# A new order for the opening of a windowed-attention and max-out FFN kernel, up to its first regular slot

## The chip, the cores and the metric

The kernel runs on one core of one Trainium2 chip. The metric is the device time of one execution in microseconds (us). The kernel before takes 179.86 us (median of three runs, 179.77 to 180.04).

A core has engines that work side by side and hand over by semaphores. PE (TensorE) multiplies matrices and transposes; its weight loads are shown apart as PEld. DVE (VectorE), ACT (ScalarE) and POOL (GpSimd) do elementwise work. SP (SyncE) issues most DMA transfers, and POOL some. Each engine executes its instructions strictly in the order in which the program issued them, so an instruction that waits also holds all that stand behind it on that engine. The results of PE go to PSUM, which has eight banks.

## The reference

Inputs are q, k, v of shape (4 batches, 8 heads, 768 positions, 64), four weight matrices in float32, a sink count of 4 and a window of 128.

```python
scores = (1 / np.sqrt(D)) * np.matmul(q, k.transpose(0, 1, 3, 2))
rel = pos[:, None] - pos[None, :]
keep = (pos[None, :] < n_sink) | ((rel >= 0) & (rel < window))
a = softmax(np.where(keep, scores, -1e9))
x = np.matmul(a, v)                      # then heads are merged: (3072, 512)
h = np.maximum(np.maximum(x @ w1, x @ w2), x @ w3)     # (3072, 768)
out = h @ w_out                                        # (3072, 512)
```

## The kernel before, in words

**Tiling.** The 3072 rows are worked on in 12 chunks of 256 positions, three for each batch. A chunk's attention looks at its own keys, at the second half of the chunk before it, and at the four sink positions of its batch (the first chunk of a batch needs neither). The eight heads are handled as four pairs, 0 to 3. "Group" 0 of K or Q holds pairs 0 and 1, group 1 holds pairs 2 and 3.

**Steps of a chunk.** Each is a small function, and `n` or `ci` is the chunk:

- `load` (L76) issues one transfer of 512 KB on SP for each of K, Q and V. There are two raw buffers for each of the three. A `gate` first writes one element of the buffer on POOL, so that the transfer waits for POOL to come to that place; `pool_gate` (L441) writes a zero there, `after(wi)` (L435) copies an element of weight matrix `wi`, and so waits for that weight to land as well.
- `cast_qk` (L95, row L101) and `cast_v` (L104, row L105) convert to bf16; K and Q have two parts for each chunk, V four.
- `turn` and `turn2` (L109, L129) transpose K or Q on PE (rows L115, L137) and copy the result from PSUM on the engine named (rows L119, L122, L141, L144). `turn_dma` (L150) does the same by transposing DMA transfers on SP: two for K (L159) and one for Q (L154). Chunks 0 to 3 are turned on PE, chunks from 4 on by DMA.
- `premask` (L252, row L257) writes an additive mask into PSUM before the scores. `score` (L260, row L275) computes the scores of a pair, `expo` (L283, row L287) the exponentials on ACT, `mask` (L290, row L293) multiplies by a 0/1 mask on DVE where there was no additive one.
- `sink_k` (POOL, L226), `sink_v` (L311), `sink_score` (L295) and `av_open` (L325) handle the four sink positions.
- `av` (L340) multiplies with V on PE (row L351) and normalises on DVE (L356, L359). `xpose` (L365, on PE, row L372) or `xpose_dma` (L376, on SP, row L378) transposes the result x for the FFN.
- `ffn_h(ci, fp, wi)` (L384) is one block of the hidden layer: 8 matmuls (row L391) for a third of the hidden columns and one of three weights. For `wi` 0 ACT copies the block out (L398), for 1 and 2 DVE takes the maximum (L402).
- `ffn_y` (L407) is the output of half a chunk: six matmuls (row L412) and a copy (L414) by DVE or, with no engine named, by ACT. `store` (L427, row L428) writes a chunk's output, 512 KB, from SP.

**Weights.** `load_w` (L236, row L239) and `load_wo` (L244) load pieces of the four weight matrices by transfers from POOL's queue, converted to bf16 on the way.

**What sets the order.** The whole program is scheduled by hand: the order of the calls is the order on every engine and every queue. L455 to L656 write out the opening, which is everything up to the transposes of chunk 3's x, one call after another. Then a loop runs over slots: slot i (from 3) holds the FFN's output of chunk i-1, its hidden layer for chunk i and the attention of chunk i+1. The branch for i = 3 (L665), the first regular slot, is written out apart; the later slots have three other branches. `RING` = 4 sets of turned K, turned Q and converted V are kept. `sinks(n)` calls `sink_k` and `sink_v` in the slot of a batch's second chunk, and `cast(n)` puts all eight casts of a chunk on POOL.

Of the kernel before, what the change touches and what calls it, by code (L numbers as in the profile page):

```python
# [16 lines left out]
def kernel(  # L17
# [13 lines left out]
    nc = tc.nc  # L31
# [11 lines left out]
    NCH = B * CPB  # L43
# [5 lines left out]
    with tc.manual_schedule():  # L49
# [404 lines left out]

        masks()  # L455
        load(0, 'k')
        cast_qk(0, 'k', 1, nc.scalar)
        warm(9)
        premask(0, (2,))
        cast_qk(0, 'k', 0, nc.vector)  # L460
        load(0, 'q')
        load(0, 'v', gate=pool_gate)
        turn(0, 'k', 0, nc.scalar)
        turn(0, 'k', 1, nc.scalar)
        sink_init()
        cast_qk(0, 'q', 1, nc.vector)
        cast_qk(0, 'q', 0, nc.vector)
        premask(0, (3,))
        turn(0, 'q', 1, nc.vector)
        premask(0, (1,))  # L470
        turn(0, 'q', 0, nc.vector)
        cast_v(0, 0, 0, nc.vector)
        masks_late()
        cast_v(0, 1, 1, nc.gpsimd)
        score(0, (2,))
        cast_v(0, 1, 0, nc.vector)
        score(0, (1,))
        load_w(0, 512, 768)
        expo(0, 2)
        load(1, 'k')  # L480
        cast_v(0, 0, 1, nc.vector)
        load_w(0, 0, 512)
        load(1, 'q')
        score(0, (3,))
        cast_qk(1, 'k', 0, nc.vector)
        expo(0, 3)
        expo(0, 1)
        premask(0, (0,))
        av_open(0)
        score(0, (0,))  # L490
        av(0, 2)
        cast_qk(1, 'k', 1, nc.gpsimd)
        av(0, 3)
        expo(0, 0)
        turn2(1, 'k', 0, nc.scalar)
        av(0, 1)
        cast_qk(1, 'q', 1, nc.gpsimd)
        load_w(1, 512, 768)
        cast_qk(1, 'q', 0, nc.vector)
        turn2(1, 'k', 1, nc.scalar)  # L500
        load_w(1, 0, 512)
        av(0, 0)
        premask(1, (1,))
        turn2(1, 'q', 0, nc.vector)
        load(1, 'v')
        turn2(1, 'q', 1, nc.vector)
        xpose(0, 0, nc.vector)
        score(1, (0,))
        score(1, (1,))
        cast_v(1, 1, 0, nc.vector)  # L510
        score(1, (2,))
        expo(1, 0)
        cast_v(1, 1, 1, nc.vector)
        xpose(0, 1, nc.vector)
        cast_v(1, 0, 1, nc.vector)
        sink_k(0)
        expo(1, 2)
        premask(1, (3,))
        sink_v(0)
        sink_score(1)  # L520
        cast_v(1, 0, 0, nc.gpsimd)
        load_w(2, 512, 768)
        mask(1, 0)
        score(1, (3,))
        expo(1, 1)
        ffn_h(0, 2, 0)
        av_open(1)
        expo(1, 3)
        mask(1, 2)
        load(2, 'k', gate=after(0, 300))  # L530
        load(2, 'q', gate=pool_gate)
        load_w(2, 0, 256)
        av(1, 0)
        av(1, 1)
        av(1, 2)
        ffn_h(0, 0, 0)
        av(1, 3)
        ffn_h(0, 1, 0)
        xpose(1, 1, nc.vector)
        xpose(1, 0, nc.vector)  # L540
        ffn_h(0, 2, 1)
        ffn_h(1, 1, 0)
        load(2, 'v', gate=after(1))
        cast_qk(2, 'k', 1, nc.vector)
        ffn_h(1, 2, 0)
        load_w(2, 256, 512)
        ffn_h(1, 0, 0)
        ffn_h(1, 2, 1)
        load(3, 'q', gate=after(0))
        ffn_h(1, 0, 1)  # L550
        cast_qk(2, 'q', 1, nc.scalar)
        load_wo(0, 3)
        load_wo(3, 6)
        cast_qk(2, 'q', 0, nc.scalar)
        ffn_h(0, 0, 1)
        ffn_h(0, 1, 1)
        cast_qk(2, 'k', 0, nc.scalar)
        ffn_h(0, 2, 2)
        turn(2, 'k', 1, nc.vector)
        load(3, 'k', gate=after(1))  # L560
        ffn_h(1, 0, 2)
        ffn_h(1, 2, 2)
        ffn_h(1, 1, 1)
        ffn_h(0, 0, 2)
        turn(2, 'q', 0, nc.scalar)
        turn(2, 'q', 1, nc.vector)
        turn(2, 'k', 0, nc.vector)
        ffn_h(1, 1, 2)
        ffn_h(0, 1, 2)
        load(3, 'v', gate=after(2))  # L570
        sink_score(2)
        cast_v(2, 0, 1, nc.gpsimd)
        score(2, (3,))
        score(2, (1,))
        score(2, (2,))
        score(2, (0,))
        expo(2, 3)
        expo(2, 0)
        expo(2, 1)
        load(4, 'k', gate=after(2))  # L580
        mask(2, 3)
        cast_v(2, 1, 0, nc.vector)
        cast_qk(3, 'q', 1, nc.gpsimd)
        cast_v(2, 1, 1, nc.gpsimd)
        ffn_y(0, 0, nc.vector)
        expo(2, 2)
        mask(2, 0)
        cast_qk(3, 'q', 0, nc.scalar)
        ffn_y(0, 1)
        cast_v(2, 0, 0, nc.vector)  # L590
        mask(2, 2)
        mask(2, 1)
        cast_qk(3, 'k', 0, nc.scalar)
        ffn_y(1, 0)
        turn(3, 'q', 1, nc.scalar)
        turn(3, 'q', 0, nc.vector)
        av_open(2)
        cast_qk(3, 'k', 1, nc.gpsimd)
        cast_v(3, 1, 0, nc.gpsimd)
        av(2, 2)  # L600
        cast_qk(4, 'k', 0, nc.gpsimd)
        av(2, 0)
        av(2, 3)
        av(2, 1)
        ffn_y(1, 1)
        load(4, 'v')
        turn(3, 'k', 0, nc.vector)
        turn(3, 'k', 1, nc.scalar)
        load(4, 'q')
        xpose(2, 0, nc.vector)  # L610
        xpose(2, 1, nc.vector)
        score(3, (1,))
        expo(3, 1)
        score(3, (3,))
        cast_qk(4, 'k', 1, nc.vector)
        cast_v(3, 0, 1, nc.vector)
        expo(3, 3)
        score(3, (0,))
        score(3, (2,))
        mask(3, 1)  # L620
        expo(3, 0)
        store(0)
        cast_v(4, 1, 0, nc.gpsimd)
        ffn_h(2, 0, 0)
        mask(3, 3)
        cast_v(3, 1, 1, nc.gpsimd)
        expo(3, 2)
        cast_v(4, 0, 0, nc.gpsimd)
        ffn_h(2, 2, 0)
        ffn_h(2, 1, 0)  # L630
# [32 lines left out]
        for i in range(3, NCH):  # L663
            n, m = i + 1, i - 1
# [194 lines left out]
```

## Time and profile before

| | us |
|---|---|
| median of the runs | 179.86 (179.77 to 180.04) |
| the profiled execution | 180.22 |
| its span in the profile | 178.4 |
| PE busy | 167.6 (94%) |
| DVE busy | 126.8 (71%) |
| ACT busy | 83.7 (47%) |
| POOL busy | 61.7 (35%) |

All times in the profile are us from the start of its span. A row of a timeline gives the start, the time it took (for merged instructions from the first start to the last end), the engine, the line, the operation, output and input, the number of instructions, and in brackets how long the engine had been idle before and what ended that. Matmuls are pipelined: a row of PE starts a little before the one ahead of it ends. SPq rows are issues; the transfer lands later. "To landing" is counted from the start of the issue.

### The profile page before, as it was taken

The numbers are of one execution on the slowest core, as the hardware profiler recorded it, in microseconds if no ns is written. First come the engines' busy times: TensorE is split into PE (matmuls) and PEld (weight loads), VectorE is DVE, ScalarE is ACT, GpSimd is POOL, SyncE is SP. The second block draws the span as 40 slices with busy tenths as digits, with TensorE's granted clock in tenths as the row PEclk, the third lists the DMA queues.
The fourth block names the chain that finished last, engine by engine and source line by source line (L and its number), as shares of the span: only waits on it lengthen the run. The fifth ranks groups of instructions, "written<-read, shape, count | busy, mean of one in ns | idle before, by whom it ended". The sixth has DMA issues, their size and how long they took to land.

```text
span 178.4 us, 4613 instructions
## 1 busy us (share of the span) xinstructions
PE 167.6 (94%) x1855; PEld 126.4 (71%) x1867; DVE 126.8 (71%) x274; ACT 83.7 (47%) x168; POOL 61.7 (35%) x118
## 2 busy tenths in 40 slices
PE   7677999999999997999999999999999999999991
PEld 2345889956786596598597697696795795796870
DVE  3499828879997895577675874884875775976451
ACT  3485732286844811932814814814616716420210
POOL 7496260054660498056064073155244000000000
PEclk9999999999999999999999999999999999999999
DMA  4999999997979999996998998999999415202203
GB/s 140 290 285 204 205 263 235 222 289 212 289 178 257 292 218 210 259 261 173 240 251 212 252 186 221 259 173 228 270 167 246 36 25 157 118 8 57 118 0 118
DMA packets 69573, 34.90 MB, mean 196 GB/s; under 512 B 26544, under 2 KB 68016, under 8 KB 69552
## 3 DMA queue, kind: packets, MB, share of 16 engines
q1 hardware_dynamic: 64912, 31.33, 78.1%
q0 software_dynamic: 4496, 3.15, 11.6%
q8 instruction: 14, 0.23, 0.6%
q10 hardware_dynamic: 144, 0.13, 0.2%
q14 instruction: 7, 0.06, 0.1%
HBM read 25.17 MB, written 6.29 MB: 176 GB/s over the span
## 4 chain that ended last, share of the span: by engine, by line
PE 74%; DVE 13%; DMA 7%; issue 2%; POOL 1%; ACT 1%; SPq 1%; POOLq 0%
PE h_ps L391 46%; PE y_ps L412 14%; PE o L351 5%; PE st L275 5%; DMA k_raw<-in_k_dram 4%; DVE e_sb L293 3%; DVE x_sb L359 3%; DMA qT<-q_bf 3%; DVE vb L105 2%; DVE h_sb L402 2%; PE o L333 1%; DVE xT L373 1%; PE sk L301 1%; PE y_ps L422 1%; DVE rc L356 1%
## 5 line engine op out<-in xcount | busy, mean ns | idle before, releaser
L391 PE MATMUL h_ps<-xT,w 128*128 128x256 bf16 x864 | 100.7, 273 | 0.0
L391 PEld LDWEIGHTS <-w 128*128 128x128 bf16 x864 | 82.2, 98 | 10.1 <-issue 0.3
L402 DVE TENSOR_TENSOR h_sb<-h_sb,h_ps 128x512 bf16<-128x512 bf16 (+1 forms) x74 | 49.0, 671 | 16.7 <-PE h_ps L391 15.2
L287 ACT ACTIVATE e_sb<-st 128x512 bf16<-128x512 f32 (+1 forms) x96 | 46.0, 579 | 8.1 <-PE st L275 8.1
L398 ACT CAST h_sb<-h_ps 128x512 bf16<-128x512 f32 x36 | 21.2, 594 | 47.4 <-PE h_ps L391 47.3
L412 PE MATMUL y_ps<-wo,h_sb 128*128 128x512 bf16 x126 | 31.5, 380 | 0.7
L105 POOL CAST vb<-v_raw 64x512 bf16<-64x512 f32 x38 | 24.7, 650 | 20.8 <-DMA v_raw<-in_v_dram 19.4
L293 DVE TENSOR_TENSOR e_sb<-e_sb,msk 128x1024 bf16<-128x1024 bf16 (+1 forms) x42 | 27.5, 690 | 1.2 <-ACT e_sb L287 1.0
L412 PEld LDWEIGHTS <-h_sb 128*128 128x128 bf16 x138 | 12.6, 98 | 15.0 <-issue 1.7
L101 POOL CAST k_bf<-k_raw 128x512 bf16<-128x512 f32 x17 | 10.2, 620 | 37.4 <-issue 23.6
L359 DVE TENSOR_TENSOR x_sb<-o,rc 128x256 bf16<-128x256 f32 x48 | 20.4, 424 | 1.6
L414 DVE COPY y_sb<-y_ps 128x512 f32<-128x512 f32 x14 | 9.7, 691 | 15.4 <-PE y_ps L412 15.2
L351 PE MATMUL o<-vb,e_sb 128*128 128x65 bf16 x352 | 16.3, 193 | 0.5 <-DVE vb L105 0.5
L351 PEld LDWEIGHTS <-e_sb 128*128 128x128 bf16 x352 | 14.3, 97 | 2.5 <-ACT e_sb L287 0.7
L275 PE MATMUL st<-qT,kT 64*128 64x128 bf16 (+1 forms) x256 | 14.3, 238 | 0.5 <-DVE qT L119 0.2
L275 PEld LDWEIGHTS <-kT 64*128 64x128 bf16 x256 | 8.6, 94 | 6.7 <-issue 4.9
L101 POOL CAST q_bf<-q_raw 128x512 bf16<-128x512 f32 x17 | 11.0, 669 | 6.6 <-DMA q_raw<-in_q_dram 6.5
L356 DVE RECIPROCAL rc<-o 128x4 f32<-128x4 f32 x48 | 8.4, 175 | 3.5 <-PE o L351 3.4
L307 ACT ACTIVATE e_sink<-sk 128x256 bf16<-128x256 f32 x8 | 3.1, 386 | 14.0 <-PE sk L301 14.0
L414 ACT COPY y_sb<-y_ps 128x512 f32<-128x512 f32 x9 | 5.4, 604 | 3.2 <-PE y_ps L412 3.0
L105 DVE CAST vb<-v_raw 64x512 bf16<-64x512 f32 x10 | 6.3, 635 | 0.2
L239 POOL DMA_DIRECT2D w<-in_moe_w_dram x7 | 5.6, 796 | 0.3 <-issue 0.3
(67 smaller groups left out, 69.1 us busy)
## 6 DMA issues: line engine op xcount, KB each, us to landing
k_raw<-in_k_dram SPq DMA_DIRECT2D x12, 512.0 KB, 5.2
q_raw<-in_q_dram SPq DMA_DIRECT2D x12, 512.0 KB, 6.1
v_raw<-in_v_dram SPq DMA_DIRECT2D x12, 512.0 KB, 7.2
out_dram<-y_sb SPq DMA_DIRECT2D x11, 512.0 KB, 3.1
w<-in_moe_w_dram POOLq DMA_DIRECT2D x5, 256.0 KB, 8.3
w<-in_moe_w_dram POOLq DMA_DIRECT2D x2, 512.0 KB, 7.9
wo<-in_moe_w_out_dram POOLq DMA_DIRECT2D x2, 384.0 KB, 11.3
kT<-k_bf SPq DMA_TRANSPOSE x16, 5.1
```

The source lines that it names most:

```text
L101: f(x[:, 2 * g:2 * g + 2].rearrange("q p i a d -> q p a i d"), y[:, 4 * g:4 * g + 4].rearrange("q (p a) i d -> q p a i d", a=2))
L105: eng.tensor_copy(vb[ci % RING][64 * i:64 * i + 64, n, :, 0:D], raws[ci, "v"][64 * n:64 * n + 64, :, i])
L275: nc.tensor.matmul(st[a][:, s:s + q1 - q0].rearrange("q n (i r) -> q n i r", i=2), lhsT=x[hp, n, p].rearrange("q i r -> q (i r)"), rhs=qc[ ...
L287: nc.scalar.activation(e[:, a, lo:], st[a][:, lo:], AF.Exp, scale=scale)
L293: (eng or nc.vector).tensor_mul(e[:, :, lo:], e[:, :, lo:], msk0 if lo else msk)
L351: nc.tensor.matmul(o[:, t, a], lhsT=e[:, a, s], rhs=vb[cv % RING][:, n, 2 * p + a], start=first, stop=True, skip_group_check=True)
L359: nc.vector.tensor_mul(xs[ci][:, :, p], o[:, :, :, 0:D], rc.unsqueeze(3).to_broadcast([128, 2, 2, D]))
L391: nc.tensor.matmul(hp[:, f].rearrange("q (i t r) -> q i t r", i=2, t=2), lhsT=w_sb[wi][:, ds, c0:c0 + 128], rhs=xTs[ci][:, :, ds].rearrang ...
L398: nc.scalar.copy(dst, hp)
L402: nc.vector.tensor_max(dst[:, x], dst[:, x], hp[:, x])
L412: nc.tensor.matmul(yp, lhsT=hs[ci][:, fb, t * 128:(t + 1) * 128], rhs=wo[:, fb], start=(fb == 0), stop=(fb == FB - 1))
L414: (nc.scalar.copy if eng is None else eng.tensor_copy)(ys[ci][:, t], yp)
```

## The change

The calls of the opening are put in another order, some casts and copies go to another engine, and the first regular slot is put in another order too. No computation is added or left out, except that the warm-up matmuls, which write a bank that nobody reads, are 4, 9 and 1 in place of 9.

The words that came with the change say that the first regular slot turns chunk 5 and then loads chunk 6, and that K and Q of chunk 5 are loaded ahead of chunk 4's turns. In the diff, `load(5, 'k')` does stand ahead of chunk 4's `turn_dma` calls and `load(5, 'q')` behind them; and in the first regular slot `load(i + 3)`, which is chunk 6, stands ahead of chunk 5's `turn_dma` calls, with `store(m)` between them.

Parts that move between engines: chunk 0's first Q and K casts and their copies; chunk 2's and chunk 3's casts and copies of turned K and Q; half of chunk 1's, chunk 2's and chunk 3's transposes of x. Over the opening, POOL has ten K/Q casts for six before, DVE four for seven, ACT six for seven. In the first regular slot the copy of the second output half goes from DVE to ACT.

The opening after the change, in its first part:

```python
        load(0, 'k')
        load(0, 'q', gate=pool_gate)
        masks()
        cast_qk(0, 'q', 1, nc.vector)
        warm(4)
        premask(0, (2,))
        premask(0, (0,))
        warm(9)
        cast_qk(0, 'k', 0, nc.scalar)
        turn(0, 'k', 0, nc.vector)
        load(0, 'v')
        cast_qk(0, 'q', 0, nc.scalar)
        turn(0, 'q', 1, nc.vector)
        sink_init()
        warm(1)
        cast_qk(0, 'k', 1, nc.gpsimd)
        cast_v(0, 1, 0, nc.vector)
        turn(0, 'k', 1, nc.scalar)
        load(1, 'k')
        turn(0, 'q', 0, nc.scalar)
        ...
        masks_late()
        ...
        load_w(0, 512, 768)
        load_w(0, 0, 512)
        ...
        cast_qk(1, 'q', 0, nc.gpsimd)
        ...
        cast_qk(1, 'q', 1, nc.gpsimd)
        load(1, 'v')
        turn2(1, 'k', 1, nc.scalar)
        expo(0, 3)
        av_open(0)
        ...
        turn2(1, 'q', 1, nc.scalar)
        ...
        expo(1, 0)
        sink_score(1)
        ...
        load(2, 'q', gate=pool_gate)
        ...
        expo(1, 2)
        ...
        expo(1, 1)
        score(1, (3,))
        ffn_h(0, 2, 0)
        mask(1, 2)
        load(2, 'k', gate=after(0, 300))
        ...
        expo(1, 3)
        load(2, 'v', gate=after(1))
        ...
        av(1, 3)
        ffn_h(0, 0, 0)
        load_w(2, 256, 512)
        xpose(1, 1, nc.vector)
        xpose(1, 0, nc.scalar)
        ffn_h(0, 2, 1)
        cast_qk(2, 'q', 0, nc.gpsimd)
        load_wo(0, 3)
        ...
```

Its end, as a diff cut to the calls on SP's queue and the transposes of chunk 3 (the rest of the stretch keeps the same kinds of calls):

```diff
+        load(5, 'k')
         ...
+        store(1)
         ...
         store(0)
         ...
         turn_dma(4, 'k')
-        store(1)
         turn_dma(4, 'q')
-        load(5, 'k')
         load(5, 'v', gate=after(0))
         load(5, 'q')
         ...
-        xpose(3, 1, nc.scalar)
-        xpose(3, 0, nc.scalar)
+        xpose(3, 0, nc.vector)
+        cast_v(4, 0, 0, nc.gpsimd)
+        xpose(3, 1, nc.scalar)
```

The first regular slot (n is 4, m is 2, i is 3), before and after:

```diff
-                sinks(n)
-                load(i + 3)
-                cast(i + 2)
-                turn_dma(i + 2, 'k')
-                turn_dma(i + 2, 'q')
-                sink_score(n)
                 score(n, (0, 1))
                 expo(n, 0)
                 expo(n, 1)
                 ffn_y(m, 0, nc.vector)
                 score(n, (2, 3))
-                mask(n, 0)
+                sinks(n)
                 mask(n, 1)
                 expo(n, 2)
-                ffn_y(m, 1, nc.vector)
+                cast(i + 2)
+                mask(n, 0)
+                sink_score(n)
+                ffn_h(i, 0, 0)
+                expo(n, 3)
+                av_open(n)
+                load(i + 3)
+                ffn_y(m, 1)
+                mask(n, 3)
+                ffn_h(i, 1, 0)
                 store(m)
+                ffn_h(i, 1, 1)
                 mask(n, 2)
-                expo(n, 3)
-                ...
+                av(n, 1)
+                ffn_h(i, 2, 0)
+                av(n, 3)
+                av(n, 0)
+                ffn_h(i, 2, 2, 1 if i + 2 < NCH else 2)
+                av(n, 2)
+                turn_dma(i + 2, 'k')
+                ffn_h(i, 0, 2)
+                turn_dma(i + 2, 'q')
+                ffn_h(i, 2, 1)
+                ffn_h(i, 1, 2)
+                xpose_dma(n)
+                ffn_h(i, 0, 1)
-                ...
```

More of the change, by code (lines that the diff above doesn't have):

```diff
@@ L561 @@
         ffn_h(1, 0, 2)
-        ffn_h(1, 2, 2)
-        ffn_h(1, 1, 1)
+        load(4, 'q')
+        sink_score(2)
+        score(2, (1,))
+        load(4, 'k', gate=after(2))
+        cast_v(2, 0, 0, nc.gpsimd)
+        score(2, (2,))
+        score(2, (3,))
+        expo(2, 3)
+        expo(2, 1)
+        ffn_h(1, 1, 2)
         ffn_h(0, 0, 2)
[L565 to L568, printed above, removed]
+        expo(2, 2)
```

282 lines of the change are left out of this document (125 added, 157 removed).

## The prediction

> **What bounds the kernel now.** I read the busy shares first, then the busy time by stretch, then the chain that ended last in order of time, and last the timelines of PE, DVE, ACT, POOL and SP around the places that the chain names. Page, part 1, and the busy time by stretch (busy us of an engine, its instructions in brackets; clock; DMA share; GB/s):
>
> ```profile
> PE 167.6 (94%) x1855; PEld 126.4 (71%) x1867; DVE 126.8 (71%) x274; ACT 83.7 (47%) x168; POOL 61.7 (35%) x118
> ...
> 10.00:20.00 10.00, 7.87 (x137) 5.58 (x134) 9.26 (x25) 7.64 (x17) 7.14 (x13) 1.00 1.29 231
> ...
> 40.00:50.00 10.00, 9.73 (x122) 7.02 (x122) 9.70 (x21) 8.18 (x19) 5.92 (x9) 1.00 0.88 228
> ...
> 100.00:120.00 20.00, 19.95 (x247) 15.99 (x248) 14.98 (x34) 9.44 (x18) 7.23 (x13) 1.00 1.20 228
> ```
>
> In the slots from 75 us on PE hardly idles (19.95 of 20 us), and the change doesn't touch them. So what matters is when slot 4 (chunk 5's scores) begins. Before it PE loses time in the opening (2.13 of the ten us shown), and once more at slot 4's start. PE's timeline, SP's, and one step of the chain that ended last:
>
> ```profile
> 66.12 3.66 PE L391 MATMUL h_ps<-xT,w 128*128 128x256 bf16 x32
> 70.74 0.29 PE L301 MATMUL sk<-qT,ks 128*32 128x256 bf16 x4 [0.97 <-DMA qT<-q_bf]
> ```
> ```profile
> 46.93 3.26 SPq L159 DMA_TRANSPOSE kT<-k_bf  x2
> ...
> 51.30 1.30 SPq L154 DMA_TRANSPOSE qT<-q_bf  x1
> 52.66 0.70 SPq L90 DMA_DIRECT2D k_raw<-in_k_dram  x1
> ...
> 59.35 2.63 SPq L90 DMA_DIRECT2D v_raw<-in_v_dram  x1
> 62.09 3.90 SPq L159 DMA_TRANSPOSE kT<-k_bf  x2
> 66.09 1.26 SPq L154 DMA_TRANSPOSE qT<-q_bf  x1
> 67.45 0.53 SPq L428 DMA_DIRECT2D out_dram<-y_sb  x1
> ```
> ```profile
> 3.38 7.12 DMA k_raw<-in_k_dram
> ```
>
> PE has finished slot 3 at 69.77 (70.74 - 0.97) and waits for chunk 5's turned Q, whose transfer was issued at 66.09. PE cannot gain from anything earlier unless this transfer comes earlier too.
>
> **The change by parts. (a) The opening.** The instructions are the same but for 14 warm-up matmuls in place of 9, and casts and copies that change engine. Rows of before, PE, DVE, ACT and POOL:
>
> ```profile
> 1.19 3.44 PE L177 MATMUL warm<-wz 128*128 128x512 bf16 x9 [1.19 <-DVE wz L166]
> ...
> 21.47 0.61 PE L372 MATMUL xt<-ident,x_sb 128*128 128x128 bf16 x8
> ```
> ```profile
> 3.14 0.39 DVE L205 MEMSET addm<- 2x128 uint32 x2
> ...
> 6.91 0.76 DVE L101 CAST q_bf<-q_raw 128x512 bf16<-128x512 f32 x2 [1.36 <-DMA q_raw<-in_q_dram]
> ```
> ```profile
> 6.04 1.07 ACT L122 COPY kT<-pt 128x512 bf16<-128x512 bf16 x2 [0.30 <-PE pt L115]
> 8.67 3.17 ACT L287 ACTIVATE e_sb<-st 128x384 bf16<-128x384 f32 x8 [1.55 <-PE st L275]
> ...
> 14.73 2.07 ACT L287 ACTIVATE e_sb<-st 128x512 bf16<-128x512 f32 x4 [1.49 <-PE st L275]
> 17.33 0.38 ACT L307 ACTIVATE e_sink<-sk 128x256 bf16<-128x256 f32 x1 [0.53 <-PE sk L301]
> ...
> 18.62 0.59 ACT L398 CAST h_sb<-h_ps 128x512 bf16<-128x512 f32 x1
> ```
> ```profile
> 9.65 1.86 POOL L239 DMA_DIRECT2D w<-in_moe_w_dram  x2
> ...
> 12.38 0.62 POOL L101 CAST q_bf<-q_raw 128x512 bf16<-128x512 f32 x1 [0.22 <-DMA q_raw<-in_q_dram]
> ```
>
> Q of chunk 0 lands at 6.9 in both orders. SP only gains the wait for a POOL memset, which is POOL's first work after the identity, and the loads behind it queue for the same bytes. The new order makes the first scores about 0.6 us later (two ACT copies, 0.54 each, now stand between Q's landing and them), but its first exponentials end at about 11 us, when K of chunk 1, ACT's next work, has only just landed (10.5, the chain's 3.38 + 7.12), so this is lost in a wait. What decides is Q of chunk 1, landed 12.4: two POOL casts at 0.62 give 13.6, its turns 0.4 more, ACT's copy 14.6, then on ACT the exponentials of pair 0 (1.04, half of 2.07) 15.7, of the sinks 16.1, of pair 2 17.15 and pair 1 18.2, the cast of the first hidden block 18.8 and pair 3 19.85. The first hidden block and three products with V run meanwhile; then the last product with V 20.1, a block 21.0, and chunk 1's PE transposes at 21.0 where they were at 21.47. Lead 0.47. The weight loads are issued behind the mask arithmetic at about 8.4 and not at 9.65. What this costs Q of chunk 1, which loads beside them, the trace doesn't show: nothing at best (the weights' first issue at 9.65 left Q its 1.9 us after K: 10.5 to 12.4), 0.5 at worst, the lead itself; I take 0.1, near the row. So the lead is 0.37, between -0.1 and 0.5. The five added matmuls stand where PE waits for Q anyhow, unless the clock stays low (rival 2).
>
> **(b) 21 to 57 us.** The same PE work, and PE full: the lead carries through, if data arrive. Chunk 2's Q and chunk 3's are now asked for before their K, and every load's gate comes about 1 us earlier. One POOL cast of chunk 2's Q is put ahead of the loads of the output weights (rival 4). In 46 to 57 us DVE is the tight engine, as the 9.70 of 10 above shows; row of DVE, and PE's rows behind it (the first serves the output blocks below):
>
> ```profile
> 54.96 1.87 DVE L402 TENSOR_TENSOR h_sb<-h_sb,h_ps 128x512 bf16<-128x512 bf16 x3
> ```
> ```profile
> 37.36 4.04 PE L412 MATMUL y_ps<-wo,h_sb 128*128 128x512 bf16 x17
> ...
> 56.88 0.38 PE L275 MATMUL st<-qT,kT 64*128 64x128 bf16 x5 [0.20 <-DVE h_sb L402]
> 57.20 1.47 PE L412 MATMUL y_ps<-wo,h_sb 128*128 128x512 bf16 x5
> ```
>
> DVE's list for this stretch keeps its masks, maxima and products; it loses one V cast (0.4 to 0.8) and one copy and receives the copy of the transposed chunk 3 at its end (0.4), with some waits for ACT. I take the last maximum at 56.8, as before, and that copy at 57.2. So DVE hands PE no lead here, but the next part uses the time.
>
> **(c) The first regular slot.** Sinks move behind all scores, and the first output block (y: six of the 17 matmuls that took 4.04 at 37.36, 1.4) now runs while DVE finishes, up to about 57.3. Before, at 57.2, PE had done the sinks (0.4, estimated from the 0.29 of four sink matmuls above) and the scores of pairs 0 and 1; now the same scores and a y block, but not the sinks: 1.4 - 0.4 - 0.1 = 0.9 ahead, and slot 3's PE work ends at 68.9, not 69.77 (bounds 68.5 and 69.4: the lead of (a) alone). Behind 57.3 stand the other scores 0.9 (0.38 for five, twelve of them), the sinks and their products 0.6, a hidden block 0.87 (a quarter of 3.66, less the pipeline's end) and the second y block 1.4: 61.05. Its copy moves from DVE to ACT and ends at about 61.7.
>
> **(d) SP's queue, which sets slot 4.** By the diff chunk 5's K is loaded ahead of chunk 4's turns; its Q is not, and chunk 6's three loads still stand ahead of chunk 5's turns. So the queue from 52.4 is V5, Q5, K6, Q6, V6, store of chunk 2, turns of K5, of Q5, then chunk 4's x. One load less, and the store (0.53 issue) moved from behind the turns to the front, where it waits for the second y copy. Transfers and their us from issue to landing, in answers cut to 55.8:56 (K6 at 55.87), 59.3:59.5 (V6), 62:64 (kT) and 66:67 (qT); the last row is the Q turn at 51.30:
>
> ```profile
> k_raw<-in_k_dram SPq DMA_DIRECT2D x1, 512.0 KB, 8.1
> ...
> v_raw<-in_v_dram SPq DMA_DIRECT2D x1, 512.0 KB, 8.2
> ...
> kT<-k_bf SPq DMA_TRANSPOSE x1, 6.0
> ...
> qT<-q_bf SPq DMA_TRANSPOSE x1, 4.6
> ...
> qT<-q_bf SPq DMA_TRANSPOSE x1, 3.5
> ```
>
> K6 lands at 64.0, V6 at 67.55 (59.35 + 8.2): 1.8 a load. The first K turn lands 0.55 after V6 and Q's turn at 70.7, 3.15 after V6. With one load less V6 lands at 65.75; the store's bytes between cost 0 to 1.8, I take 0.9, half a load, as it can be written while loads drain: Q5's turn lands at 65.75 + 0.9 + 3.15 = 69.8 (68.9 to 70.7). By issue: the store is sent by 62.25, K's turns from 62.3, and from there it is 3.26 + 3.5 = 6.8 on an empty queue (46.93, 51.30) to 4.0 + 4.6 = 8.6 as before: 69.1 to 70.9. I take 69.85, nearer to the middle of the first way as the queue is nearly drained, and 0.05 for the hand-over: 69.9. Slot 4 begins 0.8 earlier than at 70.74. PE needs chunk 4's x only some 5 us into the slot.
>
> **Sum.** -0.8 on the profiled execution's 180.22 us (span 178.4) is 179.4; the median of the runs, 179.86, is 0.36 below that execution, so the forecast is 179.05. Lowest: no wait at slot 4, 68.9, and so 178.0.
>
> **Rivals.** 1, no change: K5 and Q5's turns are as slow as before (8.6 from 62.1 to 62.3), Q5 lands at 70.7 to 70.9, and the leads of (a) and (c) only lengthen PE's wait from 0.97 to 1.8: 179.85. For it: two bounds end there. Against: less is queued in front.
>
> 2, the clock. PE's warm-up, cut shorter:
>
> ```profile
> 3.72 0.91 PE L177 MATMUL warm<-wz 128*128 128x512 bf16 x3
> 4.04 0.60 PE L177 MATMUL warm<-wz 128*128 128x512 bf16 x2
> 4.47 0.49 PE L257 MATMUL st<-addm,ident 128*128 128x384 bf16 x2
> ```
>
> Up to 3.72 six matmuls take 0.42 each ((3.72 - 1.19) / 6), from 4.04 on 0.215 ((4.47 - 4.04) / 2): PE is at half pace until about 4.0, 2.8 us after its start. In the new order four warm-ups end at 2.9 and PE idles until the mask is written at 3.53. If this gap puts the step off by as long again, to about 7, the premasks (4 at 0.32) and most of nine warm-ups at 0.42 hold PE until about 8.0, where Q's turns could start at 7.4: the scores come 0.65 later, the lead of (a) is gone and up to 0.65 of the store's time too: 179.6, no change. The Trainium skill, "TensorE: Matmul & The Clock Gate", Part 1, says that the full clock comes after a busy window of about 3.4 us that runs freely, so such a gap can cost a second window; by the rule the time would be that 179.6, by the row's early step the forecast. This trace steps after 2.8 us, so a window need not be full.
>
> 3, slower: chunk 2's store holds the turns. If PE has no lead, it stands at 57.2 with the scores of two pairs done and both y blocks still to come, 1.4 more than in (c): 62.4. ACT's copy ends at 63.05, the store is issued by 63.6, Q5's turn lands at 63.6 + 8.6 = 72.2: 1.45 late, 181.3. Turns of K5 begun after 62.15 lose at the old pace, after 63.9 even on an empty queue. For it: SP issues in order, and this wait is new. Against: the lead of (a) and (c).
>
> 4, slower: output weights late. Issues at 18.84, 23.85 and 24.6 (Q2, and the two halves; the first two answers cut to 18.84:19 and 23.85:23.9):
>
> ```profile
> q_raw<-in_q_dram SPq DMA_DIRECT2D x1, 512.0 KB, 11.4
> ...
> wo<-in_moe_w_out_dram POOLq DMA_DIRECT2D x1, 384.0 KB, 10.3
> ...
> wo<-in_moe_w_out_dram POOLq DMA_DIRECT2D x1, 384.0 KB, 12.3
> ```
>
> The second half landed at 36.9 (24.6 + 12.3), 0.4 before PE's first y block. Now POOL issues both only after Q2's cast. Asked for at 16.3, Q2 lands by 27.7 (16.3 + 11.4), and the weights, which queue behind others anyhow, lose nothing. Only if it lands as late as before, 30.2 (18.84 + 11.4), are the halves issued at 30.8 and 31.6; at 8.1 each, K6's time above, the second comes at 39.7, where the y block that begins near 37.0 wants it at 37.7 (half its 1.4 us on): PE stalls 2.0, and all behind moves with it: 181.05.
>
> **How the numbers follow.** Forecast 0.50 (178.0 to 179.45), rival 1 0.09, rival 2 0.08, rival 3 0.24, rival 4 0.09. Faster by over 0.2% (0.36 us, about what this kernel's runs can tell) 0.50, same 0.17, slower 0.33. The range 178.2 to 181.1 takes in all but the ends of the forecast's and of rival 3's bounds.
>
> **What would show it.** Right: the wait at slot 4 for chunk 5's Q at or below the 0.97, beginning near 69.9; chunk 1's transposes at 21.0; the first y block of slot 3 before 57.5; the store ahead of chunk 5's turns at about 61.7. Wrong: a new PE wait for output weights near 37, for chunk 4's turns near 55, or a store issued after 62.7.

## The result, and the profile after

The changed kernel takes 180.52 us in the median (179.98 to 181.26, 17 runs) where the kernel before, on the same chip and between the same runs, takes 179.91 (179.77 to 180.48, 17 runs). The ratio is 1.0032 with a 95% interval of 1.0019 to 1.0044: slower by about 0.6 us, where 0.8 less was forecast. Ratios are taken between the means of the runs, and a run more than 1.5% above the quickest of its kernel is left out of them (two of e5 below). The profiled execution of the changed kernel took 180.45 us (span 178.7), the one of before 180.22 (178.4). V6 stands for the load of chunk 6's V, Q5 for that of chunk 5's Q, and so on.

Busy shares and busy time by stretch, changed kernel (columns as in the prediction):

```profile
PE 169.3 (95%) x1859; PEld 126.9 (71%) x1872; DVE 123.8 (69%) x267; ACT 85.7 (48%) x171; POOL 63.9 (36%) x123
...
10.00:20.00 10.00, 9.56 (x153) 6.45 (x153) 8.66 (x26) 9.18 (x21) 5.54 (x13) 1.00 1.29 231
...
100.00:120.00 20.00, 19.95 (x246) 15.79 (x246) 14.98 (x34) 9.60 (x19) 7.68 (x12) 1.00 1.17 227
```

PE is busy for more of these ten us of the opening (9.56 with 153 instructions, before 7.87 with 137), and the later slots are untouched (19.95 of 20 in both). PE's timeline and SP's, changed kernel:

```profile
21.09 0.61 PE L372 MATMUL xt<-ident,x_sb 128*128 128x128 bf16 x8
...
56.26 1.47 PE L412 MATMUL y_ps<-wo,h_sb 128*128 128x512 bf16 x5
...
70.96 0.29 PE L301 MATMUL sk<-qT,ks 128*32 128x256 bf16 x4 [1.76 <-DMA qT<-q_bf]
```
```profile
51.02 2.62 SPq L154 DMA_TRANSPOSE qT<-q_bf  x1
53.74 0.53 SPq L90 DMA_DIRECT2D v_raw<-in_v_dram  x1
...
58.08 1.67 SPq L90 DMA_DIRECT2D v_raw<-in_v_dram  x1
61.94 0.70 SPq L428 DMA_DIRECT2D out_dram<-y_sb  x1
62.74 3.09 SPq L159 DMA_TRANSPOSE kT<-k_bf  x2
65.93 1.52 SPq L154 DMA_TRANSPOSE qT<-q_bf  x1
```

The reader is to see one thing. PE has finished slot 3 at 69.20 (70.96 - 1.76), which is 0.57 earlier than the 69.77 of before, and yet slot 4 begins 0.22 later (70.96 for 70.74): the wait for chunk 5's turned Q has grown from 0.97 to 1.76. Transfers behind it, with us from issue to landing (V6, store, first K turn, Q turn):

```profile
v_raw<-in_v_dram SPq DMA_DIRECT2D x1, 512.0 KB, 8.2
...
out_dram<-y_sb SPq DMA_DIRECT2D x1, 512.0 KB, 5.7
...
kT<-k_bf SPq DMA_TRANSPOSE x1, 5.4
...
qT<-q_bf SPq DMA_TRANSPOSE x1, 4.9
```

V6 lands at 66.28 (58.08 + 8.2), the store at 67.64 (61.94 + 5.7), the first K turn at 68.1 and the Q turn at 70.83 (65.93 + 4.9). In the kernel before these were 67.55, behind everything, 68.1 and 70.7. A load of 512 KB less stands in front, V6 is only 1.27 earlier, the store has come between, and the Q turn lands where it landed before.

**One sum for all kernels below.** From the first score matmul of slot 4 to the end of the execution there lie 180.22 - 70.74 = 109.48 us before and 180.45 - 70.96 = 109.49 after. Call this the rest. In the table "transposes" is the start of chunk 1's PE transposes, "slot 4" the start of its first score matmul.

| profiled execution | time | transposes | slot 4 | wait there | rest |
|---|---|---|---|---|---|
| before | 180.22 | 21.47 | 70.74 | 0.97 | 109.48 |
| after | 180.45 | 21.09 | 70.96 | 1.76 | 109.49 |
| after, second profile | 180.54 | 20.78 | 71.06 | 1.90 | 109.48 |
| e1, store behind the turns | 180.04 | 20.94 | 70.56 | 0.95 | 109.48 |
| e2, nine warm-ups first | 180.70 | 20.89 | 71.24 | 1.86 | 109.46 |
| e3, slot alone | 182.98 | 21.34 | 71.86 | 2.26 | 111.12 |
| e4, opening alone | 179.41 | 21.58 | 69.94 | none | 109.47 |
| e5, turn, then load | 179.83 | 21.28 | 69.33 | none | 110.50 |
| e6, e5 with Q5 ahead | 180.79 | 20.97 | 71.32 | none | 109.47 |
| e7, e3 with warm-ups | 181.65 | 21.34 | 72.15 | 0.82 | 109.50 |
| e8, e4, fewer warm-ups | 179.32 | 20.77 | 69.86 | 0.55 | 109.46 |

Apart from e3 and e5, which have reasons of their own below, the rest agrees within 0.04 us. So the time of such a kernel is told by one row, the start of slot 4. If the median runs have the same rest, slot 4 begins at 71.04 (180.52 - 109.48) in the changed kernel and at 70.43 in the one before; this is an inference, as only the runs of the table were profiled.

### The profile page after: what moved, and what is told of

Read it like the earlier page. It is cut to its first block, busy times and chain, and to the rows that moved or that the text cites. A ratio compares the mean times of both kernels' runs of the same rounds, so it can differ in the third digit from the quotient of the medians.

```text
span 178.7 us, 4624 instructions
## 1 busy us (share of the span) xinstructions
PE 169.3 (95%) x1859; PEld 126.9 (71%) x1872; DVE 123.8 (69%) x267; ACT 85.7 (48%) x171; POOL 63.9 (36%) x123
## 3 DMA queue, kind: packets, MB, share of 16 engines
q0 software_dynamic: 4496, 3.15, 11.5%
## 4 chain that ended last, share of the span: by engine, by line
PE 75%; DMA 14%; POOL 6%; issue 1%; SPq 1%; ACT 1%; DVE 0%; POOLq 0%
PE h_ps L391 46%; PE y_ps L412 15%; DMA w<-in_moe_w_dram 5%; PE st L275 5%; PE o L351 5%; DMA q_raw<-in_q_dram 3%; DMA qT<-q_bf 3%; DMA k_raw<-in_k_dram 2%; POOL k_bf L101 2%; POOL vb L105 1%; PE pt L115 1%; POOL q_bf L101 1%; PE o L333 1%; PE y_ps L422 1%; POOL msk L210 1%
## 5 line engine op out<-in xcount | busy, mean ns | idle before, releaser
L287 ACT ACTIVATE e_sb<-st 128x512 bf16<-128x512 f32 (+1 forms) x96 | 46.5, 578 | 5.1 <-PE st L275 5.0
L293 DVE TENSOR_TENSOR e_sb<-e_sb,msk 128x1024 bf16<-128x1024 bf16 (+1 forms) x42 | 28.4, 714 | 2.3 <-ACT e_sb L287 2.0
L105 POOL CAST vb<-v_raw 64x512 bf16<-64x512 f32 x38 | 24.1, 635 | 14.9 <-DMA v_raw<-in_v_dram 11.5
L101 POOL CAST k_bf<-k_raw 128x512 bf16<-128x512 f32 x17 | 11.5, 696 | 33.8 <-issue 18.2
L414 DVE COPY y_sb<-y_ps 128x512 f32<-128x512 f32 x13 | 9.0, 691 | 15.1 <-PE y_ps L412 15.0
L101 POOL CAST q_bf<-q_raw 128x512 bf16<-128x512 f32 x21 | 13.2, 655 | 13.3 <-DMA q_raw<-in_q_dram 12.5
L414 ACT COPY y_sb<-y_ps 128x512 f32<-128x512 f32 x10 | 5.9, 587 | 3.4 <-PE y_ps L412 2.2
L177 PE MATMUL warm<-wz 128*128 128x512 bf16 x14 | 5.1, 512 | 1.2 <-DVE wz L166 1.2
L101 ACT CAST k_bf<-k_raw 128x512 bf16<-128x512 f32 x5 | 3.1, 626 | 6.2 <-POOL v_raw L438 3.5
```

Of the source, the lines that this page charges most:

```text
L101: f(x[:, 2 * g:2 * g + 2].rearrange("q p i a d -> q p a i d"), y[:, 4 * g:4 * g + 4].rearrange("q (p a) i d -> q p a i d", a=2))
L105: eng.tensor_copy(vb[ci % RING][64 * i:64 * i + 64, n, :, 0:D], raws[ci, "v"][64 * n:64 * n + 64, :, i])
L287: nc.scalar.activation(e[:, a, lo:], st[a][:, lo:], AF.Exp, scale=scale)
L293: (eng or nc.vector).tensor_mul(e[:, :, lo:], e[:, :, lo:], msk0 if lo else msk)
L414: (nc.scalar.copy if eng is None else eng.tensor_copy)(ys[ci][:, t], yp)
```

## The experiments

**Theory and rivals.** The theory of the queue (theory S in the expectations): chunk 2's store, now ahead of chunk 5's turns on SP, holds the Q turn, while the new opening by itself is a gain. Theory O: the opening itself is worse, because its split warm-up puts off the full clock (the prediction's rival 2). Two more came with the results: theory C, that a wait of some 2 us at slot 4 makes PE lose its clock, and theory W, that the nine warm-ups hold up the opening and so cost time.

**e1: the store behind the turns.** The changed kernel with one call moved.

```diff
                 ffn_h(i, 1, 0)
-                store(m)
                 ffn_h(i, 1, 1)
                 ...
                 turn_dma(i + 2, 'q')
+                store(m)
                 ffn_h(i, 2, 1)
```

> The changed kernel with one call moved: the store of chunk 2 stands behind chunk 5's turns on SP and not ahead of them. Theory S (the store ahead of the turns sets slot 4): the turns of K5 are issued from about 59.8, when V6's issue ends, Q5's turn lands 3.2 us after V6 (66.3), at about 69.5, and slot 4 begins at 69.3 to 69.6 in place of 70.96: median about 179.1, faster than before by 0.4%. Theory O (the clock's late step in the opening sets the time, the turns only follow PE): the wait goes away but runs still spread over 1.3 us, and the median lies between 179.5 and 180.2. If the transposes are slow by themselves, Q5's turn still lands near 70.8 and the median stays at 180.5.

Measured: 179.60 us (179.22 to 180.04, 12 runs) with 180.0 for before measured beside it (179.77 to 180.33, 19 runs); ratio 0.9974 (0.9964 to 0.9985). SP's timeline of e1, and the landings of V6 and of the Q turn:

```profile
51.48 2.62 SPq L154 DMA_TRANSPOSE qT<-q_bf  x1
...
59.00 2.56 SPq L90 DMA_DIRECT2D v_raw<-in_v_dram  x1
61.67 3.91 SPq L159 DMA_TRANSPOSE kT<-k_bf  x2
65.68 1.27 SPq L154 DMA_TRANSPOSE qT<-q_bf  x1
```
```profile
v_raw<-in_v_dram SPq DMA_DIRECT2D x1, 512.0 KB, 8.1
...
qT<-q_bf SPq DMA_TRANSPOSE x1, 4.7
```

The Q turn lands 3.3 behind V6 (65.68 + 4.7 = 70.4; 59.00 + 8.1 = 67.1), as before (3.15); with the store between it was 4.55 (70.83 - 66.28). So the store's place costs the Q turn 1.25 to 1.4 us here, although the profiled run of e1, its slowest, has V6 0.8 later. One call makes the changed kernel faster than before; between the two ratios lie 0.58%, 1.04 us. The theory's number was missed, though: it put slot 4 at 69.3 to 69.6 and the median at 179.1, and the profile shows 70.56 with a wait of 0.95 left, since V6 landed at 67.1 where the theory had 66.3.

**e2: nine warm-ups first.** The changed kernel with the warm-ups of 4 and 9 exchanged.

```diff
-        warm(4)
+        warm(9)
         premask(0, (2,))
         premask(0, (0,))
-        warm(9)
+        warm(4)
```

> The changed kernel with nine warm-up matmuls ahead of the premasks and four behind, in place of four and nine, so that PE has no gap before 3.5 us. Theory O: the step to full pace comes back to about 4.0 in each run, Q's turns begin at 7.35 and not 7.75, the runs come together (within 0.5 us), and with the store's issue moving along the median falls to about 180.0. Theory S alone: the profile's slot 4 moves by at most 0.4, the median stays within 0.3 of 180.5.

Measured: 181.13 (180.63 to 182.57, 8 runs); ratio 1.008 (1.005 to 1.011). Chunk 1's transposes come at 20.89, 0.2 earlier than in the changed kernel, and slot 4 comes later:

```profile
71.24 0.29 PE L301 MATMUL sk<-qT,ks 128*32 128x256 bf16 x4 [1.86 <-DMA qT<-q_bf]
```

So the split warm-up is not what costs the time, and theory O falls: PE's lead in the opening doesn't reach slot 4. The theory of the queue, too, is off here: it left at most 0.3 from 180.5. Why this order is slower than the changed one is open; three of the eight runs, at 182.36 to 182.57, have a mean granted clock of 0.991 where the others have 1.0 (see e3 and e7).

**e3: the slot alone.** The opening of before with the changed slot 3 (lines 667 to 701 of the changed kernel in place of 665 to 699).

> The kernel before with the first regular slot of the changed one. Theory S: the store now stands ahead of the turns while K5, V5, Q5 and chunk 6 are as late as before, so V6 lands at 67.5, the store 1.35 later and Q5's turn 3.2 behind it, near 72.1: slot 4 1.3 late, median about 181.2. Theory O: the opening is that of before, so the time is that of before within 0.3, 179.6 to 180.2.

Measured: 182.92 (181.4 to 183.19, 6 runs); ratio 1.015 (1.0124 to 1.0176). V6 lands at 67.2 (58.88 + 8.3), the store is sent at 62.33, and the Q turn lands at 71.67 (66.97 + 4.7). PE's timeline and its busy time by stretch (us, PE, PEld, DVE, ACT and POOL busy, then the granted clock):

```profile
71.86 0.29 PE L301 MATMUL sk<-qT,ks 128*32 128x256 bf16 x4 [2.26 <-DMA qT<-q_bf]
72.08 1.46 PE L275 MATMUL st<-qT,kT 64*128 64x128 bf16 x18
```
```profile
72.00:73.00 1.00, 1.00 (x18) 0.79 (x16) 0.00 (x0) 0.61 (x2) 0.00 (x0) 0.53 1.15 225
73.00:74.00 1.00, 1.00 (x12) 0.42 (x7) 0.00 (x0) 1.00 (x3) 0.00 (x0) 0.50 0.43 98
74.00:75.00 1.00, 1.00 (x4) 0.33 (x3) 0.00 (x0) 1.00 (x3) 0.00 (x0) 0.50 0.94 274
75.00:76.00 1.00, 1.00 (x5) 0.38 (x4) 0.05 (x1) 0.82 (x2) 0.00 (x0) 0.76 1.17 334
```

This is more than the wait. Behind a wait of 2.26 us PE is granted half its clock: the eighteen score matmuls take 1.46 where they took 0.84 before, and the clock column gives about 3.4 us of it (0.94 in the first us, two whole ones, 0.48 in the last). Half of 3.4 us is lost, 1.7, and the rest is indeed 111.12 for 109.48, 1.64 more. Five of the six runs have a mean clock of 0.991 and take 182.74 to 183.19; the sixth, with a clock of 1.0, takes 181.4, near the 181.2 expected. Slot 4 is 1.12 late, for 1.3 expected.

**e4: the opening alone.** The changed opening with slot 3 of before, so load 6 first, the turns ahead of the store, both output copies on DVE.

> The changed opening with the first regular slot of before (store behind the turns, both y blocks copied on DVE). Theory S: Q5's turn lands near 69.5, PE ends slot 3 between 69.2 and 69.8, so slot 4 begins near 69.7: median about 179.1 to 179.3. Theory O: the spread of 1.3 us stays, median about 180.2 to 180.5.

Measured: 179.15 (178.94 to 179.41, 5 runs); ratio 0.9954 (0.9942 to 0.9967). By the median it is the fastest of all kernels here, and beats both. PE's timeline, SP's, and the landings of V6 and the Q turn:

```profile
69.94 0.29 PE L301 MATMUL sk<-qT,ks 128*32 128x256 bf16 x4
```
```profile
51.57 1.33 SPq L154 DMA_TRANSPOSE qT<-q_bf  x1
53.00 0.53 SPq L90 DMA_DIRECT2D v_raw<-in_v_dram  x1
...
57.66 2.62 SPq L90 DMA_DIRECT2D v_raw<-in_v_dram  x1
60.39 3.93 SPq L159 DMA_TRANSPOSE kT<-k_bf  x2
64.41 1.26 SPq L154 DMA_TRANSPOSE qT<-q_bf  x1
65.76 0.53 SPq L428 DMA_DIRECT2D out_dram<-y_sb  x1
```
```profile
v_raw<-in_v_dram SPq DMA_DIRECT2D x1, 512.0 KB, 8.2
...
qT<-q_bf SPq DMA_TRANSPOSE x1, 3.2
```

No bracket stands at slot 4: the Q turn has landed at 67.6, 2.3 before PE wants it. (That is 1.75 behind V6; with the same order on SP e8 below has 3.29, so part of this margin is this execution's luck.) Two things differ from the changed kernel. The turns are issued from 60.39, behind V6 alone. And chunk 4's Q turn takes SP 1.33 where it takes 2.62 in the changed kernel, so V5 goes out at 53.00 and not at 53.74, and V6 lands at 65.86. The transposes come at 21.58, later than before: the gain of this kernel is the queue's, not that of a PE lead in the opening.

The two halves of the change add up: the ratio of the opening alone, 0.9954, times that of the slot alone where it keeps its clock (e7 below), 1.0077, is 1.0031, and the changed kernel has 1.0032. Of the 0.78% between e4 and the changed kernel the store's place is 0.58% (e1). The 0.2% left to the rest of the slot's order is not taken apart.

**e5: the order of the change's words.** Slot 3 with chunk 5's turns ahead of chunk 6's loads, the store behind both.

```diff
                 av_open(n)
+                turn_dma(i + 2, 'k')
+                turn_dma(i + 2, 'q')
                 load(i + 3)
                 ...
-                store(m)
                 ...
-                turn_dma(i + 2, 'k')
                 ffn_h(i, 0, 2)
-                turn_dma(i + 2, 'q')
+                store(m)
```

> The changed kernel with the first regular slot in the order that the words of the change name: chunk 5's turns ahead of chunk 6's load, the store behind both. Theory S: Q5's cast is done at about 61.2, its turn is issued near 61.3 on a drained queue and lands by 65.5, so PE waits for nothing at slot 4, which begins when slot 3's work ends, near 69.2: median 178.5 to 178.9, faster than before by 0.6 to 0.8%. If the transposes or chunk 6's later loads make a new wait instead, slot 4 or slot 5 begins late and the median is 179.1 or above.

Measured: 181.77 (179.59 to 182.6, 12 runs) with 180.06 for before measured beside it (179.67 to 180.52, 17 runs); ratio 1.0054 (1.0023 to 1.0084). The profiled run took 179.83, with slot 4 at 69.33 and no wait there, as expected; what follows it is 110.50 for 109.48, with PE waits of 0.20 for slot 4's x and 0.46 for chunk 6's K in it. So the profile fits the theory and the median does not: 178.5 to 178.9 was forecast. Three runs take 179.59 to 179.83, the others 181.22 and more; the two longest, 182.5 and 182.6, have a mean clock of 0.991, the rest 0.999 or 1.0. Three more profiles of the same kernel were taken to see one of the longer runs.

> The order of the change's words once more (chunk 5's turns, then chunk 6's loads, the store behind both). Its quick runs take 179.6 to 179.8, most take 181.2 or more. If the extra 1.5 is the late queue behind chunk 6's loads, a longer run shows PE waits of 1.0 or more for the x turn of slot 4 (near 74) or for the turns of chunk 6 (near 83). If it is the opening, the wait stands before 60, at chunk 4's Q turn. If it is the clock, the granted clock shows a half-pace stretch of about 3.4 us behind one of these waits.

> The same kernel as in the two looks before it (179.83 and 179.56, slot 4 at 69.3), for one of its longer runs. Behind slot 4's first score matmul lie 109.48 in nearly every profile, 110.3 to 110.5 in the two looks. A longer run (181.2 or more) with slot 4 at 71.7 or later has its wait at or before slot 4 (chunk 4's Q turn); with slot 4 near 69.3, 111.9 or more lie behind it and the wait is at slot 4's x turn or at chunk 6's turns.

> As the run before it, which it repeats: a longer run shows whether its time lies ahead of slot 4's first score matmul or behind it; a quick one has slot 4 near 69.3 and 110.3 to 110.5 behind it.

Measured: 179.56, 180.81 and 179.84. Slot 4 begins at 69.31, 69.16 and 69.36 without a wait; behind it lie 110.25, 111.65 and 110.48. None of the longest was caught, but the second of these is 1 us longer than its fellows. Its PE timeline, and the chain that ended last up to slot 4's x (start, us, what):

```profile
75.54 1.69 PE L391 MATMUL h_ps<-xT,w 128*128 128x256 bf16 x14 [1.66 <-DMA xT<-x_sb]
```
```profile
54.25 7.04 DMA q_raw<-in_q_dram
...
61.34 1.55 POOL q_bf L101 x2
```
```profile
62.92 1.23 SPq L154 DMA_TRANSPOSE qT<-q_bf  x1
64.20 0.57 SPq L90 DMA_DIRECT2D k_raw<-in_k_dram  x1
...
66.73 1.90 SPq L428 DMA_DIRECT2D out_dram<-y_sb  x1
68.72 3.03 SPq L378 DMA_TRANSPOSE xT<-x_sb  x1
```

Q of chunk 5 lands late (61.3), POOL casts it until 62.9, its turn goes out then, and all that now stands behind the turn on SP, three loads, the store and chunk 4's x, goes out as much later. The x turn takes 6.8 us to landing, at 75.5, and PE waits 1.66 for it. The wait at slot 4 is gone, and another stands five us behind it. That the runs of 181.2 to 181.9 are the same thing at a larger size is likely but not shown; in the two longest some half pace comes on top.

**e6: as e5, with chunk 5's Q asked for right behind its K.**

```diff
         load(5, 'k')
+        load(5, 'q')
         ...
-        load(5, 'q')
```

> As the run before, and chunk 5's Q is loaded right behind its K, ahead of chunk 4's turns, as the words say. Theory S: nothing more to gain, since Q5's turn already has 3 us to spare: same within 0.2 us of the run before, or later by up to 0.8 if the 1.8 us of Q5's bytes delay chunk 4's turns, which PE reaches at about 55.7: then PE shows a wait for a turn of chunk 4 there, and the median is 0.3 to 0.8 above.

Measured: 181.65 (180.79 to 183.48, 6 runs); ratio 1.0096 (1.006 to 1.0133). PE's timeline:

```profile
57.94 0.61 PE L275 MATMUL st<-qT,kT 64*128 64x128 bf16 x12 [2.68 <-DMA qT<-q_bf]
```

The load that is put ahead makes chunk 4's turns late: SP issues chunk 4's Q turn only at 53.06 (51.02 in the changed kernel), and PE waits 2.68 us for it. So the second half of the change's words, taken literally, moves the wait one chunk forward, as the expectation had it; but by the median this kernel is no slower than e5 (181.65 and 181.77), where 0.3 to 0.8 more was expected. Five of its six runs have a mean clock of 0.977 to 0.991. The profiled one is the sixth, with a clock of 1.0: in it PE kept its full pace through the wait of 2.68 us.

**e7: e3 with warm-ups in the wait.** Eight more warm-up matmuls behind slot 3's last block; they write the bank that nobody reads.

```diff
                 ffn_h(i, 0, 1)
+                warm(8)
```

> The run with the first regular slot alone, with eight warm-up matmuls (1.73 us at full pace) put on PE behind slot 3's last block, where it waits 2.26 us for Q5's turn. They write a bank that nobody reads. Theory C (the idle wait lets the clock gate halve PE's clock for 3.41 us, at a loss of about 1.5 us, in most runs): no run shows half clock, the mean clock is 0.995 or above in all, and the median falls from 182.92 to 181.2 to 181.5, the time of the one run of that kernel that kept its clock. If the half clock comes from something else, most runs still show a mean clock of 0.991 and the median stays near 182.9.

Measured: 181.61 (181.16 to 181.66, 6 runs); ratio 1.0077 (1.0061 to 1.0093). All runs have a mean clock of 0.996 or more. Slot 4's first matmuls, in PE's timeline:

```profile
72.15 0.29 PE L301 MATMUL sk<-qT,ks 128*32 128x256 bf16 x4 [0.82 <-DMA qT<-q_bf]
72.37 0.84 PE L275 MATMUL st<-qT,kT 64*128 64x128 bf16 x18
```

The Q turn is no earlier than in e3 (slot 4 at 72.15), but the score matmuls take 0.84 again, and the rest is 109.50. With PE kept busy the kernel is 1.31 us faster than e3: theory C holds for this wait, and what is left of e3's loss is the late Q turn.

**e8: e4 with fewer warm-ups,** `warm(4)` in place of `warm(9)`.

> The opening alone with four warm-up matmuls in place of nine behind the premasks. Theory W (how late PE's full clock comes, 3.9 to 7.8 us in the six profiles, decides how long nine warm-ups hold up chunk 0's turns): chunk 0's turns begin at 7.4 at the latest in any run, chunk 1's transposes by 21.0, and the median falls from 179.15 to 178.6 to 178.9 with the slowest run below 179.1. If the warm-ups are hidden anyway, the median stays at 179.1 to 179.2.

Measured: 179.31 (179.11 to 179.66, 6 runs); ratio 0.9958 (0.9944 to 0.9973), no better than e4. PE's timeline:

```profile
20.77 0.61 PE L372 MATMUL xt<-ident,x_sb 128*128 128x128 bf16 x8
...
55.83 0.29 PE L301 MATMUL sk<-qT,ks 128*32 128x256 bf16 x4 [0.46 <-DMA qT<-q_bf]
...
69.86 0.29 PE L301 MATMUL sk<-qT,ks 128*32 128x256 bf16 x4 [0.55 <-DMA qT<-q_bf]
```

The transposes come 0.81 earlier than in e4, but PE gives that back at the Q turns of chunks 4 and 5 (0.46 and 0.55), and slot 4 is 0.08 earlier. Theory W falls: a lead in the opening is worth nothing as long as the turns set the pace.

**The changed kernel, a second profile.**

> The changed kernel once more, to see one of its longer runs. If the time above the first profile's 180.45 is made at slot 4 by chunk 5's Q turn, a run of 180.9 or more shows the first score matmul of slot 4 at 71.4 or later with a wait of 2.0 or more on that DMA. If it is made elsewhere (chunk 4's Q turn, the output weights, a later slot), the wait at slot 4 stays near 1.8 and another PE wait on a DMA of 0.5 or more stands in the page.

Measured: 180.54, near the median of its 17 runs. PE's timeline and waits:

```profile
71.06 0.29 PE L301 MATMUL sk<-qT,ks 128*32 128x256 bf16 x4 [1.90 <-DMA qT<-q_bf]
```
```profile
PE sk L301 <- DMA qT<-q_bf: 1.9, 1, 1.9
...
PE st L275 <- DMA qT<-q_bf: 0.6, 1, 0.6
```

Both waits that the expectation names are there. The transposes are 0.31 earlier than in the first profile (20.78) and slot 4 is 0.10 later: the Q turns of chunks 4 and 5 take the lead and more. The run was not one of 180.9 or more, so what the longest runs of the changed kernel look like is not seen. Half pace is not what makes them long: the three above 181 have a mean clock of 1.0.

## Why the prediction was wrong, point by point

**What bounds the kernel: right.** Chunk 5's turned Q sets slot 4, and with the rest at 109.48 it sets the time.

**(a) The opening: right in its number, without weight.** The transposes came at 21.09, forecast 21.0, and at 20.78 in the second profile. Part of this is luck: in eight profiles with this opening unaltered they come between 20.78 and 21.58. What I carried on from it, a lead that is worth time, was wrong as long as a turn is awaited: e2, e8 and the second profile had transposes 0.2 to 0.8 earlier than their fellows and no earlier slot 4 to speak of, and e4 is fastest with transposes at 21.58.

**(b) 21 to 57 us: right.** The last maximum and the copy of the transposed chunk 3 in DVE's timeline of the changed kernel end at 56.8 and 57.1, forecast 56.8 and 57.2. Rival 4's wait for output weights near 37 isn't in the list of PE's waits. The other sign of being wrong, a wait for chunk 4's turns near 55, is not in this profile but in the second one (0.6).

```profile
54.90 1.87 DVE L402 TENSOR_TENSOR h_sb<-h_sb,h_ps 128x512 bf16<-128x512 bf16 x3
56.70 0.42 DVE L373 COPY xT<-xt 128x512 bf16<-128x512 bf16 x1
```

**(c) The first regular slot: right within 0.3.** The first output block begins at 56.26, before 57.5 as forecast; slot 3's PE work ends at 69.20, forecast 68.9 (bounds 68.5 to 69.4). The second output copy, in ACT's timeline, ends at 61.92, forecast 61.7:

```profile
61.33 0.59 ACT L414 COPY y_sb<-y_ps 128x512 f32<-128x512 f32 x1 [0.18 <-ACT e_sb L287]
```

**(d) SP's queue: here it failed,** by the sizes of two terms. The sum was 65.75 (V6's landing) + 0.9 (the store's bytes) + 3.15 = 69.8. Measured was 66.28 + 4.55 = 70.83, so 0.53 and 0.50 more.

The table has the nine profiles with chunk 6's loads ahead of chunk 5's turns (issue start plus us to landing; the latter are rounded to 0.1).

| profile | chunk 4's Q turn holds SP | V6 lands | store lands | Q turn lands | behind V6 | behind the store |
|---|---|---|---|---|---|---|
| before | 1.30 | 67.55 | after the turn | 70.69 | 3.14 | |
| after | 2.62 | 66.28 | 67.64 | 70.83 | 4.55 | 3.19 |
| after, second profile | 2.62 | 66.36 | 67.69 | 70.90 | 4.54 | 3.21 |
| e1 | 2.62 | 67.10 | after the turn | 70.38 | 3.28 | |
| e2 | 2.66 | 66.52 | 67.91 | 71.08 | 4.56 | 3.17 |
| e3 | 1.43 | 67.18 | 68.53 | 71.67 | 4.49 | 3.14 |
| e4 | 1.33 | 65.86 | after the turn | 67.61 | 1.75 | |
| e7 | 1.30 | 67.45 | 68.84 | 72.05 | 4.60 | 3.21 |
| e8 | 2.64 | 66.57 | after the turn | 69.86 | 3.29 | |

The first is V6's landing. "One load less ahead" was worth 1.27 and not 1.8. The prediction has V5 first in the queue from 52.4 on, and SP got to it only at 53.74: chunk 4's Q turn took SP 2.62 where it had taken 1.30. In e4 it took 1.33, V5 went out at 53.00 and V6 landed 0.42 earlier than in the changed kernel. I had taken V6's landing without any bound. The length of that one issue goes with the opening: in the eleven profiles with the changed opening (e2, e6 and e8, which alter a line of it, included), it is 2.6 to 2.8 where the transposes come by 21.09, 2.0 where they come at 21.12 to 21.28, and 1.3 from 21.37 on, and it always ends 1.0 to 1.1 us behind the landing of the first of the two stores ahead of chunk 4's turns (52.51 in the changed kernel, 51.86 in e4). So PE's lead in the opening comes with a later queue; why that store lands later is open.

The second is the store. From both ends, 0 and 1.8, I took 0.9, since the store might be written while loads drain. The store cost about 1.4 (4.55 - 3.15), and e1, where it stands behind the turns, has 3.3 again. In all five profiles with the store ahead, the store lands 1.33 to 1.39 behind V6 and the Q turn 3.1 to 3.2 behind the store, as it lands 3.1 to 3.3 behind V6 in three of the four without (e4 is the exception). So the store costs the turn its whole transfer, nothing of it is hidden, and that transfer is 1.35 and not a load's 1.8. The trace of before already had this size: there the store lands 1.26 behind the Q turn ahead of it (67.45 + 4.5 = 71.95; 70.69). The Trainium skill, "DMA: Bandwidth & Descriptors", section "Queues, rings and completion order", says that each DMA engine takes the descriptors of a ring in ring order; the landings here agree with that.

The prediction's second way, by issue, had the answer inside its bounds (69.1 to 70.9), but I leaned to the first way's middle, 69.8, because "the queue is nearly drained". It was not: when the changed kernel issues the turns at 62.74, Q6 (56.22 + 8.4 = 64.6), V6 and the store are still to land. And its 6.8 "on an empty queue" was read at 46.93, where a store was still on its way until 49.96 (42.56 + 7.4).

So what happened is rival 1 by its place and size (Q5 at 70.7 to 70.9, the wait grown to 1.8; I gave it 0.09 and a time of 179.85, 0.67 below the median), by a part of rival 3's mechanism, the store ahead of the turns: not late, at 61.94 for a forecast of 62.25 at the latest, but with its bytes. The profiles differ by +0.23, as their slots 4 do (+0.22). The medians differ by +0.61: the profiled execution of before lies 0.31 above its median, that of the changed kernel 0.07 below. I had subtracted the gain from the longer execution and then moved to the median, which was right in form, but it supposes that slot 4 scatters alike in both kernels. The runs of before spread over 0.7 us, the changed ones over 1.3. That the later scatter is that of a longer chain, output copy, store, turns, is argued and not shown.

**Rival 2, the clock.** The late step was there, but nothing shows that the gap makes it. PE's warm-up in the changed kernel:

```profile
1.20 1.89 PE L177 MATMUL warm<-wz 128*128 128x512 bf16 x4 [1.20 <-DVE wz L166]
...
4.85 2.85 PE L177 MATMUL warm<-wz 128*128 128x512 bf16 x9
```

Nine warm-ups took 2.85 us, 0.32 each, between the 0.42 at half pace and the 0.215 at full pace of the prediction, and held PE until 7.7 (8.0 in the rival). But e3 and e7 have the opening of before, without the gap, and there the first nine warm-ups take 4.02 us for 3.44 in the profile of before: the step comes late in some executions and not in others. And it cost nothing at slot 4: in the second profile the nine take 2.29 us and slot 4 is no earlier, nor is it in e8.

**The forecast's 0.8 was in the change, but in the other half.** The opening alone brings it: slot 4 at 69.94 (forecast 69.9), 179.15 us (forecast 179.05). There V6 lands at 65.86, forecast 65.75, with the turns right behind it. That the numbers meet is luck: the forecast had slot 4 wait for a turn that lands at 69.8, and in e4 the turn lands at 67.61 and slot 4 begins when PE's work ends. The slot's new order, which I had counted as a lead of 0.9 on PE, brings PE no time at slot 4 and costs the queue 1.4.

## What to carry to other kernels

Where one queue carries loads, turns and stores, list its contents in order ahead of the transfer that PE waits for, and give every transfer ahead of it its whole time, a store too; each term of that sum needs a bound, the issue times of turns among them. When a wait for a DMA ends a stage, a lead of the engines before it only lengthens the wait, so ask of each part of a change whether it moves that transfer. And where a profile's rest behind one instruction is the same in every kernel, compare that one row and not the whole.

## What the runs showed of the hardware that I had not expected

Behind a wait of 2.26 us PE was granted half its clock in the profile of e3 (five of its six runs have the mean clock that goes with it), and the half pace then lasted about 3.4 us and cost 1.6, nearly as much as the wait itself; eight matmuls that nobody reads, put into the wait, prevented it (e7). The length of the wait alone does not decide: waits of 1.76 to 1.90 in the profiles of the changed kernel and of e2 left the clock at full pace, and so did one of 2.68 in the profile of e6. The Trainium skill, "TensorE: Matmul & The Clock Gate", Part 1, puts the fall behind at least one idle window of about 3.4 us, and lets the window run freely; the length of the half pace in e3 agrees with that, but the wait of e3 is shorter than one such window, and there the measurement decides.

A DMA turn's landing isn't a constant: chunk 5's Q turn took 3.2 us from issue to landing in e4, 4.6 to 4.9 before, after and in e1, with a V6 transfer of 8.1 to 8.2 ahead of it. What makes the difference is open.
